# Attention and SwiGLU on one core: reordering the first batch's loads, preparations and products

## Chip, cores, metric

One core of a Trainium2 chip. The time is the device time of one execution in microseconds (us), median over executions. A profile's span is about 1.7 us shorter than the time of the same execution.

## The reference

Causal attention with a forget-like bias for 8 batches of 8 heads (576 positions, head size 64), then a SwiGLU block on the 4608 rows of 512 that result:

```python
scores = scale * np.matmul(q, k.transpose(0, 1, 3, 2))
cum = np.cumsum(np.maximum(s, 0.0), axis=-1)
bias = -(cum[:, :, :, None] - cum[:, :, None, :])
scores = np.where(causal, -1000000000.0, scores + np.minimum(bias, 0.0))
attn = softmax(scores)                      # exp of the maximum taken off, over the sum
x = np.matmul(attn, v) -> (4608, 512)
out = (silu(x @ w_gate) * (x @ w_val)) @ w_out      # 512 -> 1536 -> 512
```

## The kernel before

Heads come in 16 blocks of four ("block 2" is heads 8 to 11). A block is loaded as f32, cast to bf16, transposed by TensorE (blocks 0 to 4; later ones go through a DMA transpose) and copied from PSUM into `KQ`. A head then takes four score pieces (PE), exponentials (ACT), two causal selects (POOL), value products (PE), a division (DVE), and per pair of heads a transpose into `xt`. The heads of batch 0 run first, alone. From then on FFN tile `tt` and the heads of batch `tt+1` are interleaved step by step by `pump`. `SP` issues most loads, POOL the weight loads.

```python
def second_psum():                 # after the first batch: 2 wide + 4 single banks -> 8 single banks
    at_end = dict(released)
    first_psum.close()
    psb = ctx.enter_context(tc.tile_pool(name="psb", bufs=1, space=PSUM))
    ...

def side(h, step):                 # beside head 4*h+step
    bh = HB * h + step
    if bh == 8:  w_load("o", 0)
    if bh == 10: w_load("o", 1)
    if bh == H:                    # V of batch 1, f32 -> bf16, on POOL
        for c in range(5): cast_v(1, c, nc.gpsimd)
    ...
    if h + 2 < NHB and h + 2 >= NPE:
        if step == 1: cast_one(h + 2, "k", nc.gpsimd)
        if step == 2: cast_one(h + 2, "q", nc.gpsimd); scratch(h + 2)
        ...

def prep_one(hb, i):               # a quarter of a block: transposes, then two copies out of one bank
    g, nm = divmod(i, 2)
    nm = ("k", "q")[nm]
    pe_transpose(hb, nm, g)
    pe_out(hb, nm, g, 0, nc.vector)
    pe_out(hb, nm, g, 1, nc.scalar)

def first_batch():
    avq = {4: (0,), 5: (1, 2), 6: (3, 4), 7: (5, 6, 7)}
    wq = {0: ("g", 0), 1: ("v", 0), 3: ("g", 1), 5: ("v", 1)}
    for h in range(H):
        for ci in range(4): score_piece(h, ci)
        if h in wq: w_load(*wq[h])
        ...                        # block 1's transposes at h == 1, V 0's casts at h == 2 and 3
        for p in avq.get(h, ()):
            av_piece(p, range(NCH)); av_out(p)
            if p % 2 == 0 and p: x_pe(p // 2 - 1)
    ...
    load_v(1, range(5)); load_qk(3); load_qk(4)
    x_pe(H // 2 - 1)

hook = {                           # FFN tile 0, by step
    1: [lambda: cast_one(2, "k", nc.gpsimd), lambda: cast_one(2, "q", nc.vector)],
    2: [lambda: prep_one(2, 0)], ..., 5: [lambda: prep_one(2, 3)],
    8: [casts of block 3 on gpsimd], 21: [lambda: load_qk(5)],
}
n0 = 7 if tt == 0 else 0           # heads of batch 1 start after this step
```

The softmax here doesn't subtract the row's maximum and nothing guards it: scores larger than these inputs give would overflow.

## Time and profile before

| | us |
|---|---|
| median (3 runs, 407.97 to 409.79) | 408.16 |
| span of the profiled run | 406.5 |
| first score / first FFN matmul / last matmul's end | 11.93 / 34.40 / 402.78 |
| lost by TensorE: 34.40 to 46.5 / 46.5 to 65 / 65 to 75 / from 75 on | 4.2 / 4.15 / 0 / 4.45 |

"Lost" is the length of a stage less the time which its matmuls need at full clock, back to back; the prediction tells how the need was worked out. It counts half-clock time and small waits that "busy" hides. The lines themselves are in the prediction.

### The profile page before, as it was taken

Reading aid. Unit: us, or ns where it says so; the run is one execution under the profiler, and the core shown is the slowest. Engines: PE = TensorE matmul, PEld = TensorE weight load, DVE = VectorE, ACT = ScalarE, POOL = GpSimd, SP = SyncE. Lnnn points to the kernel's source line nnn. Section 1 sums busy time; section 2 is a strip of 40 time slices with the busy share of each in tenths; the row PEclk is TensorE's granted clock in tenths of the full one; section 3 lists DMA queues with packets and bytes.
Section 4 is the critical chain, followed back from the end, with each engine's and each line's share of the span. In section 5 each row is a group of like instructions: output and inputs, shape, how many; then the busy total and the mean of one; then the engine's idle time right before and its main releaser. Section 6 shows DMA issues by size and latency. Waiting matters only on the chain.

```text
span 406.5 us, 8052 instructions
## 1 busy us (share of the span) xinstructions
PE 384.8 (95%) x3100; PEld 213.0 (52%) x3100; DVE 249.1 (61%) x487; ACT 212.0 (52%) x407; POOL 125.0 (31%) x225
## 2 busy tenths in 40 slices
PE   2778799999999999999999999999999999999996
PEld 2664355655555555555555555555555554444442
DVE  7755658547863696368835784489447733852760
ACT  6742566855555655555545654655555542322321
POOL 6852444732442235222613162316211110000000
PEclk9988899999999999999999999999999999999999
DMA  7999899398635784579356944681510002002002
GB/s 242 188 250 212 267 192 269 133 272 190 178 93 194 174 206 118 173 194 211 102 157 192 247 72 127 214 167 51 120 57 0 2 27 78 0 16 89 2 1 103
DMA packets 85288, 56.71 MB, mean 140 GB/s; under 512 B 65489, under 2 KB 69553, under 8 KB 85249
## 3 DMA queue, kind: packets, MB, share of 16 engines
q1 hardware_dynamic: 81440, 51.44, 47.0%
q0 software_dynamic: 3808, 4.76, 6.9%
q8 instruction: 24, 0.39, 0.4%
q14 instruction: 16, 0.12, 0.1%
HBM read 37.90 MB, written 15.93 MB: 132 GB/s over the span
## 4 chain that ended last, share of the span: by engine, by line
PE 89%; DVE 4%; ACT 2%; DMA 2%; POOL 1%; issue 1%; ACTq 0%; SPq 0%
PE bank L546 23%; PE bank L518 22%; PE bank L533 22%; PE bank L347 9%; PE bank L385 7%; PE bank L420 3%; PE wide L347 1%; DMA kq<-HL 1%; PE one L385 1%; DMA s_sb<-in_s_dram 1%; ACT th L523 1%; POOL vt L171 1%; DVE pp L525 1%; DVE kq L301 1%; ACT pt L360 1%
## 5 line engine op out<-in xcount | busy, mean ns | idle before, releaser
L360 ACT ACTIVATE pt<-bank 128x512 bf16<-128x512 f32 x224 | 104.2, 505 | 42.4 <-PE bank L347 35.1
L525 DVE SCALAR_TENSOR_TENSOR pp<-th,bank 128x512 bf16<-128x512 bf16 x108 | 74.2, 687 | 65.2 <-ACT th L523 64.6
L518 PE MATMUL bank<-xt,wg 128*128 128x512 bf16 x432 | 112.1, 382 | 0.7 <-DVE xt L425 0.7
L533 PE MATMUL bank<-xt,wv 128*128 128x512 bf16 x432 | 112.5, 383 | 0.0
L523 ACT ACTIVATE th<-bank 128x512 bf16<-128x512 f32 x108 | 64.5, 597 | 81.6 <-PE bank L518 79.8
L546 PE MATMUL bank<-wo,ht 128*128 128x512 bf16 x432 | 105.7, 379 | 0.0
L363 POOL TENSOR_SCALAR_AFFINE_SELECT pt<-pt 128x512 bf16<-128x512 bf16 x64 | 40.8, 638 | 127.1 <-ACT pt L360 124.7
L538 DVE TENSOR_TENSOR ht<-pp,bank 128x512 bf16<-128x512 bf16 x108 | 73.8, 684 | 7.4
L347 PE MATMUL bank<-kq 128*128 128x128 bf16 (+4 forms) x504 | 66.7, 241 | 3.3 <-DVE kq L301 2.5
L347 PEld LDWEIGHTS <-kq 128*128 128x128 bf16 x576 | 46.1, 100 | 40.2 <-issue 4.2
L518 PEld LDWEIGHTS <-wg 128*128 128x128 bf16 x432 | 38.6, 98 | 36.9 <-issue 1.9
L533 PEld LDWEIGHTS <-wv 128*128 128x128 bf16 x432 | 38.9, 99 | 35.2 <-issue 1.7
L546 PEld LDWEIGHTS <-ht 128*128 128x128 bf16 x432 | 38.1, 98 | 34.9
L385 PEld LDWEIGHTS <-pt 128*128 128x128 bf16 x960 | 41.1, 98 | 19.0 <-issue 1.9
L385 PE MATMUL bank<-vt,pt 128*128 128x65 bf16 x840 | 44.0, 194 | 0.0
L554 ACT ACTIVATE ysb<-bank 128x512 f32<-128x512 f32 x36 | 21.5, 597 | 42.9 <-PE bank L546 41.4
L368 POOL TENSOR_SCALAR_AFFINE_SELECT pt<-pt 128x64 bf16<-128x64 bf16 x64 | 15.3, 239 | 63.4 <-ACT pt L360 60.7
L402 DVE TENSOR_TENSOR ot<-bank,rc 128x320 bf16<-128x320 f32 x56 | 27.5, 492 | 1.9
L424 DVE COPY xt<-bank 128x128 bf16<-128x128 bf16 (+6 forms) x28 | 9.0, 321 | 31.7 <-PE bank L420 31.0
L401 DVE RECIPROCAL rc<-bank 128x5 f32<-128x5 f32 x56 | 10.6, 190 | 25.2 <-PE bank L385 25.2
L171 POOL CAST vt<-rawv 128x512 bf16<-128x512 f32 (+1 forms) x40 | 25.8, 673 | 0.0
L230 POOL CAST ck<-rawk 128x1152 bf16<-128x1152 f32 x15 | 17.4, 1159 | 11.5 <-DMA rawk<-in_k_dram 11.5
(59 smaller groups left out, 191.6 us busy)
## 6 DMA issues: line engine op xcount, KB each, us to landing
out_dram<-ysb SPq DMA_DIRECT2D x36, 256.0 KB
rawk<-in_k_dram SPq DMA_DIRECT2D x15, 576.0 KB
rawq<-in_q_dram SPq DMA_DIRECT2D x15, 576.0 KB
rawv<-in_v_dram SPq DMA_DIRECT2D x32, 256.0 KB
ks<-ck SPq DMA_DIRECT2D x11, 288.0 KB
qs<-cq SPq DMA_DIRECT2D x11, 288.0 KB
wg<-in_moe_w_gate_dram POOLq DMA_DIRECT2D x2, 768.0 KB, 12.0
wv<-in_moe_w_val_dram POOLq DMA_DIRECT2D x2, 768.0 KB, 13.6
```

The source lines that it names most:

```text
L171: eng.tensor_copy(VT[b % 2][0:n, c, :, 0:D], loaded["v", b][0:n, c, :, :])
L347: nc.tensor.matmul(sc[:, o : o + w], T[:, 1, e * S + 128 * tj : e * S + 128 * (tj + 1)], T[:, 0, e * S + lo : e * S + hi], start=True, sto ...
L360: nc.scalar.activation(pt[:, c0 : c0 + W], sc[:, 0:W], AF.Exp, scale=0.125)
L363: nc.gpsimd.affine_select(pt[:, 1088:1600], pt[:, 1088:1600], pattern=[[0, 4], [1, 128]], compare_op=ALU.is_ge, fill=zreg, base=0, channel ...
L385: nc.tensor.matmul(av[:, bi * (D + 1) : (bi + 1) * (D + 1)], pt[:, c0 : c0 + 128], VT[b % 2][:, tj, h, :], start=(tj == 0), stop=(tj == bi),)
L402: nc.vector.tensor_mul(ot[:, :, e * D : (e + 1) * D], av3[:, :, 0:D], rc[:, :, None].to_broadcast([128, NCH, D]),)
L518: nc.tensor.matmul(pg, WG[j][:, c, f0 : f0 + 128], xt[:, c, :], start=(c == 0), stop=(c == 3),)
L523: nc.scalar.activation(th, pg, AF.Tanh, scale=0.5)
L525: nc.vector.scalar_tensor_tensor(pp, in0=th, scalar=1.0, in1=pg, op0=ALU.add, op1=ALU.mult)
L533: nc.tensor.matmul(pv, WV[j][:, c, f0 : f0 + 128], xt[:, c, :], start=(c == 0), stop=(c == 3),)
L538: nc.vector.tensor_mul(ht, pp, pv)
L546: nc.tensor.matmul(py, hts[ft][:, ts_ * 128 : (ts_ + 1) * 128], WO[ft // WKO][:, ft % WKO, :], start=(ft == 0), stop=(ft == NFT - 1),)
```

## The change

The intent is to bring the first batch's work into a better order, so that TensorE has no long wait ahead of its steady part: (1) weight loads later, behind V 0, in halves; (2) k and q of block 3 loaded ahead of V 1; (3) heads 0 to 5 score before the first value product, and in the next batch the value products follow the scores by up to three heads; (4) half of block 2 is prepared in the first batch; smaller: casts and memsets shared out otherwise, score rows of later blocks issued by POOL, stores one step later. Its core:

```diff
         def first_batch():
-            avq = {4: (0,), 5: (1, 2), 6: (3, 4), 7: (5, 6, 7)}
-            wq = {0: ("g", 0), 1: ("v", 0), 3: ("g", 1), 5: ("v", 1)}
+            avq = {5: (0,), 6: (1, 2), 7: (3,)}
+            wq = {
+                2: (("g", 0, 0), ("v", 0, 0)),
+                3: (("g", 0, 1), ("v", 0, 1)),
+                5: (("g", 1),),
+                6: (("v", 1),),
+            }
@@ (V 0's casts: c 0 to 2 on POOL at h == 3, c 3 and 4 on DVE at h == 1)
+                    load_qk(3)
+                if h == 6:
+                    cast_one(2, "k", nc.gpsimd)
+                if h == 7:
+                    aug(3, SP4)
+                    load_v(1, range(5))
+                    load_qk(4)
@@
+            cast_one(2, "q", nc.gpsimd)
+            w_load("o", 0)
+            w_load("o", 1)
+            x_pe(0)
+            for p in (4, 5, 6, 7):
+                av_piece(p, range(NCH))
+                av_out(p)
+                ...
+                if p >= 6:
+                    nm = ("k", "q")[p - 6]
+                    pe_transpose(2, nm, 0)
+                    for r in range(2):
+                        pe_out(2, nm, 0, r, nc.scalar)
+            x_pe(3)
@@
-            1: [lambda: cast_one(2, "k", nc.gpsimd), lambda: cast_one(2, "q", nc.vector)],
-            2: [lambda: prep_one(2, 0)],
-            3: [lambda: prep_one(2, 1)],
-            4: [lambda: prep_one(2, 2)],
-            5: [lambda: prep_one(2, 3)],
+            1: [lambda: prep_one(2, 2)],
+            2: [lambda: prep_one(2, 3)],
@@
-            n0 = 7 if tt == 0 else 0
+            n0 = 4 if tt == 0 else 0
@@ side()
-            if bh == 8:
-                w_load("o", 0)
-            if bh == 10:
-                w_load("o", 1)
-            if bh == H:
+            if bh == H + 2:
                 for c in range(5):
                     cast_v(1, c, nc.gpsimd)
@@ attn_items()
+        AV_AT = {H: (), H + 1: (), H + 2: (), H + 3: (H,), H + 4: (H + 1, H + 2), H + 5: (H + 3, H + 4)}
```

More of the change, by code (lines that the diff above doesn't have):

```diff
@@ L95 @@
     s_sb = const.tile([BH, S], FP32)
-    one_s = const.tile([BH, S], FP32)
+    one_s = const.tile([128, 1], FP32)
     c8 = const.tile([BH, S], FP32)
@@ L190, with init_vt @@
         nc.sync.dma_start(s_sb, s.rearrange("b h n -> (b h) n"))
+        def init_vt(i):
+            nc.gpsimd.memset(VT[i][:, :, :, D : D + 1], 1.0)
+            nc.gpsimd.memset(VT[i][64:128, 4, :, 0:D], 0.0)
         for r in range(NR):
@@ L196 @@
         nc.vector.memset(warm, 0.0)
+        nc.vector.memset(one_s, 1.0)
         nc.scalar.activation(warm, warm, AF.Exp)
-        nc.vector.memset(one_s, 1.0)
         nc.vector.memset(HL[:, 0:2, 0, :].bitcast(FP32), ONES2)
@@ L201, with pads @@
         make_identity(nc, ident)
+        def pads(i):
+            for r in range(2):
+                nc.gpsimd.memset(KQ[i][r][64 * r : 64 * r + 64, :, NR * S :], 0.0)
         for r in range(2):
-            nc.gpsimd.memset(aug_rows(0, r), 0.0)
+            nc.gpsimd.memset(aug_rows(0, r)[:, 1, :], 0.0)
             nc.scalar.mul(
-                KQ[1][r][64 * (1 - r) : 64 * (1 - r) + 64, 0, :],
-                one_s[:, 0:1].to_broadcast([64, NR * S + 64]), 0.0,
-            )
-        for r in range(2):
-            nc.gpsimd.memset(aug_rows(1, r)[:, 1, :], 0.0)
-            for i in range(2):
-                nc.gpsimd.memset(KQ[i][r][64 * r : 64 * r + 64, :, NR * S :], 0.0)
+                KQ[0][r][64 * (1 - r) : 64 * (1 - r) + 64, 0, :],
+                one_s[0:64, 0:1].to_broadcast([64, NR * S + 64]), 0.0,
+            )
+        pads(0)
+        init_vt(0)
+        init_vt(1)
+        nc.vector.memset(aug_rows(1, 0), 0.0)
+        nc.gpsimd.memset(aug_rows(1, 1), 0.0)
+        pads(1)
         nc.vector.tensor_scalar(s_sb, s_sb, 0.0, 8.0, ALU.max, ALU.mult)
-        nc.vector.tensor_tensor_scan(c8, one_s, s_sb, 0.0, ALU.mult, ALU.add)
+        nc.vector.tensor_tensor_scan(
+            c8, one_s[0:BH, 0:1].to_broadcast([BH, S]), s_sb, 0.0, ALU.mult, ALU.add
+        )
         nc.vector.tensor_copy(HL[:, 0, 1, :], c8)
@@ L219 @@
         SP4 = [nc.sync] * 4
+        GP4 = [nc.gpsimd] * 4
         cts = {}
@@ L304, in pe_out, with w_load @@
                 give(tp[1])
-        def w_load(kind, j):
+        def w_load(kind, j, h=None):
             dst = {"g": WG, "v": WV, "o": WO}[kind][j]
@@ L313, in w_load @@
                 w = moe_w_gate if kind == "g" else moe_w_val
-                src_ap = w[:, j * WCH : (j + 1) * WCH].rearrange("(c p) n -> p c n", p=128)
+                lo, hi = (0, WCH) if h is None else (h * WCH // 2, (h + 1) * WCH // 2)
+                src_ap = w[:, j * WCH + lo : j * WCH + hi].rearrange("(c p) n -> p c n", p=128)
+                dst = dst[:, :, lo:hi]
             nc.gpsimd.dma_start(dst, src_ap)
@@ L408, in av_out, with x_tiles @@
             pts.pop(bh)
+        def x_tiles(b, r):
+            for tt in ((0, 1) if b == 0 else (b + 1,)):
+                if r == 0:
+                    xts[tt] = xtp.tile([128, 4, TT], BF16, tag="xt", name="xt")
         def x_pe(pr):
@@ L412, in x_pe @@
             ot = ots.pop(pr)
-            for tt in ((0, 1) if b == 0 else (b + 1,)):
-                if r == 0:
-                    xts[tt] = xtp.tile([128, 4, TT], BF16, tag="xt", name="xt")
+            x_tiles(b, r)
             bs = take()
@@ L440, in side @@
                 if step == 0:
+                    transposes(h + 1)
+                    aug(h + 1, GP4)
+                if step == 2:
                     split(h + 1, "k", nc.vector)
-                    aug(h + 1, SP4)
-                if step == 1:
+                if step == 3:
                     split(h + 1, "q", nc.vector)
@@ L449, in side @@
                     cast_one(h + 2, "q", nc.gpsimd)
+                if step == 3:
                     scratch(h + 2)
-                if step == 3:
-                    transposes(h + 2)
             bn = h // 2 + 1
@@ L475, in prep_one @@
             pe_out(hb, nm, g, 1, nc.scalar)
-        PREP_AT = {(0, 3): 0, (1, 3): 1, (2, 1): 2, (2, 3): 3}
+        PREP_AT = {
+            2: {(1, 3): 0, (2, 1): 1, (2, 3): 2, (3, 1): 3},
+            3: {(0, 3): 0, (1, 3): 1, (2, 1): 2, (2, 3): 3},
+        }
+        AV_AT = {H: (), H + 1: (), H + 2: (), H + 3: (H,), H + 4: (H + 1, H + 2), H + 5: (H + 3, H + 4)}
+        X_AT = {H + 3: (), H + 5: (H + 1,), H + 6: (H + 3,), H + 7: (H + 5,)}
         def attn_items():
@@ L486, in attn_items @@
                     if step == 0 and 3 < h + 1 < NPE:
-                        aug(h + 1, SP4)
+                        aug(h + 1, GP4)
                     for ci in range(4):
@@ L492, in attn_items @@
                         yield kk + 0.1 + ci / 8
-                        if h + 1 < NPE and (step, ci) in PREP_AT:
-                            prep_one(h + 1, PREP_AT[step, ci])
+                        if (step, ci) in PREP_AT.get(h, ()):
+                            prep_one(h + 1, PREP_AT[h][step, ci])
                             yield kk + 0.1 + ci / 8
-                x = kk - 2
-                if x >= H and x % 2 == 1:
-                    x_pe(x // 2)
-                    yield kk + 0.5
-                p = kk - 1
-                if H <= p < BH:
-                    av_piece(p, (0, 1, 2))
-                    yield kk + 0.6
-                    av_piece(p, (3,))
-                    yield kk + 0.7
-                    av_piece(p, (4,))
-                    av_out(p)
-                    yield kk + 0.8
+                for x in X_AT.get(kk, (kk - 2,)):
+                    if x % 2 == 1 and H <= x < BH:
+                        x_pe(x // 2)
+                        yield kk + 0.5
+                for p in AV_AT.get(kk, (kk - 1,)):
+                    if H <= p < BH:
+                        av_piece(p, (0, 1, 2))
+                        yield kk + 0.6
+                        av_piece(p, (3,))
+                        yield kk + 0.7
+                        av_piece(p, (4,))
+                        av_out(p)
+                        yield kk + 0.8
+        stores = []
         def ffn_items(tt):
@@ L512, in ffn_items @@
             hts = []
+            for f in stores:
+                f()
+            stores.clear()
             for ft in range(NFT):
@@ L555, in ffn_items @@
                 give(ybs)
-                nc.sync.dma_start(
-                    out[tt * TT + ts_ * 128 : tt * TT + (ts_ + 1) * 128, :], ysb
-                )
+                for f in stores:
+                    f()
+                stores.clear()
+                stores.append(
+                    lambda a=tt * TT + ts_ * 128, y=ysb: nc.sync.dma_start(
+                        out[a : a + 128, :], y
+                    )
+                )
+                if tt == NTT - 1:
+                    stores.pop()()
                 yield 1
-        def init_vt(i):
-            nc.gpsimd.memset(VT[i][:, :, :, D : D + 1], 1.0)
-            nc.gpsimd.memset(VT[i][64:128, 4, :, 0:D], 0.0)
         cast_half(0, "k", 0, nc.scalar)
-        cast_half(0, "q", 0, nc.gpsimd)
+        cast_half(0, "q", 0, nc.scalar)
         aug(0, SP4)
@@ L569 @@
         load_qk(2)
-        aug(1, [nc.gpsimd] * 4)
         for nm in ("k", "q"):
@@ L576 @@
         pe_out(0, "q", 0, 0, nc.vector)
-        pe_out(0, "q", 1, 0, nc.scalar)
+        pe_out(0, "q", 1, 0, nc.vector)
         cast_half(0, "k", 1, nc.scalar)
-        cast_half(0, "q", 1, nc.vector)
+        cast_half(0, "q", 1, nc.gpsimd)
+        aug(1, GP4)
         for nm, eng in (("k", nc.scalar), ("q", nc.vector)):
@@ L583 @@
                 pe_out(0, nm, g, 1, eng)
-        cast_one(1, "k", nc.gpsimd)
+        cast_one(1, "k", nc.vector)
         cast_one(1, "q", nc.vector)
-        init_vt(0)
         def first_batch():
-            avq = {4: (0,), 5: (1, 2), 6: (3, 4), 7: (5, 6, 7)}
-            wq = {0: ("g", 0), 1: ("v", 0), 3: ("g", 1), 5: ("v", 1)}
+            avq = {5: (0,), 6: (1, 2), 7: (3,)}
[4 more added lines that the diff above has]
+                6: (("v", 1),),
+            }
             for h in range(H):
@@ L593, in first_batch @@
                     score_piece(h, ci)
-                if h in wq:
-                    w_load(*wq[h])
+                for w in wq.get(h, ()):
+                    w_load(*w)
                 if h == 1:
@@ L602, in first_batch @@
                             pe_out(1, nm, g, r, nc.vector)
-                if h == 2:
+                    for c in range(3, 5):
+                        cast_v(0, c, nc.vector)
+                if h == 3:
                     for c in range(3):
                         cast_v(0, c, nc.gpsimd)
-                if h == 3:
-                    for c in range(3, 5):
-                        cast_v(0, c, nc.gpsimd)
                     aug(2, SP4)
+                    load_qk(3)
[5 more added lines that the diff above has]
+                    load_qk(4)
                 for p in avq.get(h, ()):
@@ L612, in first_batch @@
                     av_out(p)
-                    if p % 2 == 0 and p:
-                        x_pe(p // 2 - 1)
-            init_vt(1)
-            aug(3, SP4)
-            load_v(1, range(5))
-            load_qk(3)
-            load_qk(4)
-            x_pe(H // 2 - 1)
+            cast_one(2, "q", nc.gpsimd)
[4 more added lines that the diff above has]
+                av_piece(p, range(NCH))
+                av_out(p)
+                if p == 5:
+                    x_pe(1)
+                if p == 6:
+                    x_pe(2)
+                if p >= 6:
+                    nm = ("k", "q")[p - 6]
+                    pe_transpose(2, nm, 0)
+                    for r in range(2):
+                        pe_out(2, nm, 0, r, nc.scalar)
+            x_pe(3)
         first_batch()
@@ L632, in pump @@
                     state["pos"] = 1e9
-        LAG = 1.65
+        LAGS = [0] + [1.65] * NTT
         hook = {
-            1: [lambda: cast_one(2, "k", nc.gpsimd), lambda: cast_one(2, "q", nc.vector)],
-            2: [lambda: prep_one(2, 0)],
-            3: [lambda: prep_one(2, 1)],
-            4: [lambda: prep_one(2, 2)],
-            5: [lambda: prep_one(2, 3)],
-            8: [lambda: cast_one(3, "k", nc.gpsimd), lambda: cast_one(3, "q", nc.gpsimd)],
+            1: [lambda: prep_one(2, 2)],
+            2: [lambda: prep_one(2, 3)],
+            7: [lambda: cast_one(3, "k", nc.gpsimd), lambda: cast_one(3, "q", nc.gpsimd)],
             21: [lambda: load_qk(5)],
@@ L644 @@
         for tt in range(NTT):
-            lo = H * (tt + 1) + (LAG if tt else 0)
-            hi = min(H * (tt + 2) + LAG, BH + 2)
+            lo = H * (tt + 1) + LAGS[tt]
+            hi = min(H * (tt + 2) + LAGS[tt + 1], BH + 2)
             span = 36
-            n0 = 7 if tt == 0 else 0
+            n0 = 4 if tt == 0 else 0
             n = 0
```

## The prediction

> **What bounds the kernel now.** I read the page's slices first, then busy time by stage, then what TensorE waited for, then the timelines of PE and POOL over the first 60 us. The slices say where to look:
>
> ```profile
> PE   2778799999999999999999999999999999999996
> POOL 6852444732442235222613162316211110000000
> PEclk9988899999999999999999999999999999999999
> DMA  7999899398635784579356944681510002002002
> ```
>
> A slice is about 10.2 us. PE is under 90% only in slices 1 to 5 and the last, and PEclk is low in 3 to 5. The stages, cut at the first score (11.93), the first FFN matmul (34.40) and the end of the long wait (46.51):
>
> ```profile
> core 0: us, PE busy (x) PEld busy (x) DVE busy (x) ACT busy (x) POOL busy (x), PEclk, DMA share, GB/s
> 11.93:34.40 22.47, 15.97 (x231) 12.66 (x232) 15.04 (x35) 12.52 (x16) 15.56 (x31) 0.92 1.15 230
> 34.40:46.51 12.11, 9.59 (x51) 4.39 (x51) 6.69 (x11) 4.03 (x7) 1.15 (x1) 0.87 1.04 266
> 46.51:65.00 18.49, 17.06 (x141) 9.88 (x142) 11.62 (x20) 12.94 (x26) 10.91 (x17) 0.91 1.00 191
> 75.00:402.80 327.80, 327.75 (x2543) 176.14 (x2541) 199.61 (x393) 166.56 (x334) 84.59 (x150) 1.00 0.45 120
> ```
>
> From 75 us on TensorE has no gap. Busy is not the same as full speed, so I took starts instead: in the steady part each kind of matmul starts a fixed time after the last one (512 columns 0.216 us, 128 columns 0.056, the 65-column value product 0.029). Multiplying these by the counts in each stage gives the time that the work needs at full speed. From 34.40 to the last matmul's end (402.78) are 368.4 us for 355.6 us of need: 12.8 us are lost, 4.5 of them spread over 75 to 403 (1.4%) and 8.3 between 34.40 and 65 (4.2 to 46.51, 4.1 after). Between 12 and 34.40 the need is 11.4 us out of 22.4. So what can be won is ahead of 65 us; afterwards TensorE's own work sets the end. The waits of PE from 34.3 to 75:
>
> ```profile
> PE bank L347 <- DVE kq L301: 2.5, 1, 2.5
> PE bank L518 <- DVE xt L425: 0.7, 1, 0.7
> PE bank L347 <- DVE pp L525: 0.6, 1, 0.6
> PE bank L272 <- DVE ot L402: 0.4, 1, 0.4
> PE bank L420 <- DVE ot L402: 0.3, 1, 0.3
> ```
>
> One wait, 2.5 us at head 8's first score, stands out: k and q of head block 2 are cast only after the first batch (at 32.6 on POOL and 37.6 on DVE), then go through four transposes and eight copies that alternate with the FFN's DVE work. The first batch itself is paced by a chain over POOL and PE:
>
> ```profile
> 20.84 0.76 POOL L315 DMA_DIRECT2D wg<-in_moe_w_gate_dram  x1
> 21.60 1.18 POOL L171 CAST vt<-rawv 128x512 bf16<-128x512 f32 x2
> ...
> 30.86 0.64 POOL L363 TENSOR_SCALAR_AFFINE_SELECT pt<-pt 128x512 bf16<-128x512 bf16 x1 [2.02 <-ACT pt L360]
> 31.44 0.24 POOL L368 TENSOR_SCALAR_AFFINE_SELECT pt<-pt 128x64 bf16<-128x64 bf16 x1
> ```
> ```profile
> 22.28 0.31 PE L385 MATMUL one<-vt,pt 128*128 128x65 bf16 x5 [1.77 <-POOL vt L171]
> 22.83 0.19 PE L385 MATMUL one<-vt,pt 128*128 128x65 bf16 x1 [0.24 <-POOL vt L171]
> ...
> 34.40 1.86 PE L518 MATMUL bank<-xt,wg 128*128 128x512 bf16 x4 [0.70 <-DVE xt L425]
> 36.06 1.74 PE L533 MATMUL bank<-xt,wv 128*128 128x512 bf16 x4
> ...
> 37.92 1.03 PE L518 MATMUL bank<-xt,wg 128*128 128x512 bf16 x4
> ```
>
> The V casts stand behind a weight issue on POOL; the value product of head 0 waits for them and, in PE's order, holds the scores of head 5 back; so ACT idles 2.0, 1.85 and 1.3 us before the last three pairs of exponentials (PE's turn alternates with value products), and the last causal select ends at 31.7. From there to the FFN's first matmul are 2.7 us (value product, DVE, transpose, DVE). That first pair of matmul groups then takes 1.66 us each from start to start, against 0.86 later.
>
> [...] three spans of 3.41 us at half clock, from 23.9, 34.1 and 47.7, each after a stretch in which PE worked about half the time or less. At full demand such a window costs up to 1.7 us. [...] DMA share is 1.15 in the first batch, and the third issue of V 1 takes 4.3 us on SP while the weights are moving.
>
> **The change, part by part.** (a) Start: POOL's cast of q goes to ACT, one cast of k to DVE, memsets are shared out. The first score waits for the chain s load, five DVE operations to 8.16, 3.6 us of DMA, so it stays at 11.9; 0 us.
>
> (b) First batch. Order on PE: heads 0 to 5 score before the first value product. ACT, at 1.64 us a head from 13.0, can run to head 5's end at about 23. POOL then becomes the pace, because it now issues six weight DMAs, not four (halves cost an issue each, 0.78), and casts k of block 2 (1.15) before head 7's select. I add its list: three selects to 18.4; two issues to 20.0; select of head 3 to 20.85; two issues to 22.4; three V casts (0.58 each) to 24.2; selects 4 and 5 to 25.9; issue 26.6, select 6 27.5, issue 28.2, cast k 29.4, select 7 30.2. Head 6's scores stand behind value product 0, thus behind 24.2; its exponentials run 25.1 to 26.7 and head 7's to about 28.8, so POOL, not ACT, ends last. With the same 2.7 us tail the FFN starts at 33.0, **1.4 us earlier**. The weights' first halves, issued at 18.4 and 19.2, need 0.4 MB each at the 115 to 200 GB/s seen: before 28, not in the way.
>
> (c) Block 2: half of its transposes (10 x 0.056 = 0.56 us of need) moves into the batch's idle PE time: **0.6 us**. Its casts are done before the FFN, the other half is at the FFN's first two steps, and head 8 scores after the fifth step, about 5 us in. DVE and ACT copies (0.7 each, one after the other here) with tanh and products between them end at about +4.6 us. The 2.5 us wait goes, and with it the half-clock window that followed at 47.7 (1.7): **4.2 us**.
>
> (d) Value products of heads 8 to 12 come three heads later, so PE no longer meets `ot` and the select closely: the waits of 0.4 and 0.3 go, some of the 0.6 may. Against that, scores take banks sooner: I reckon that the third gate product waits some 0.7 us for a bank held until DVE's product. In the gate and value part of this tile I add DVE 12 x 1.37 + 6 x 0.77 + 5 x 0.7 + 1.2 = 25.7 us beside about 28.5 of PE, so about a microsecond more of small waits is likely. Net **0.5 us**.
>
> (e) FFN's opening at half clock costs 1.5 us now. PE is denser in front of it in the new order, but still waits for the last select; even odds: **0.75 us**.
>
> (f) Later: score rows issued from POOL, stores one step later, transposes given one step more. No PE wait there now, so 0.
>
> Sum: 1.4 + 0.6 + 4.2 + 0.5 + 0.75 = 7.45, with 0.3 for the rest of the 8.3: 7.75. 408.16 - 7.75 = 400.4 us, 1.9% less.
>
> **Rivals.** *A new wait in front of the FFN.* POOL gets 14.5 us of work between 13 and 30.2 and hardly idles; if an issue or cast runs longer, FFN starts as late as before and the gain is only (c) to (e), some 402 to 403. For it: POOL's order; against: the durations are steady in the trace.
>
> *V 1 or a weight arrives late.* wo is now issued at 32, not at 49 and 58, behind wg 1 and wv 1, and takes engines from V 1, which crept while weights moved (issued 30.7, last piece at 43). I put V 1 at about 48 and its use, value product of head 8, at about 53; k and q 4 follow at some 50. If V 1 takes until 55, PE stops 2 to 3 us: 403 to 405. wv 1 is due at 47 and should land by 44.
>
> *Full gain.* Clock stays full at the FFN's opening and no bank wait appears: 397 to 398.
>
> *Steady state.* If POOL's extra issues or the later splits open gaps after 75 us, the gain is eaten; DVE has 61% and POOL 26% load there, so I give it little.
>
> **Range and chances.** 400.4, with 397.0 for the full gain and 404.0 for a late transfer. The 2% line is at 400.0, just beside the middle: faster 0.45, same 0.53, slower 0.02.
>
> **What would show it right or wrong.** In the new profile: first score still at 11.9 (a); POOL without idle from 18.4 to 30 and FFN's first matmul near 33.0 (b); PE's wait for DVE `kq` gone and half-clock windows down from three to one or two (c, e); no wait on `rawv`, `wv` or `rawk` that reaches PE in 35 to 65 us; from 70 us the same 1.4% loss. A first FFN matmul after 34, a PE wait over 1 us between 35 and 65, or a gap after 75 would make it wrong on the slow side; an FFN start before 32 on the fast side.

## The result

405.15 us median (4 runs, 405.01 to 405.92) against 408.28 us for the kernel before on the same chip. The ratio is 0.992, interval 0.9892 to 0.9947: about 3 us less, where 7.75 were predicted, and outside the range. (Ratios here and below are the mean time of one kernel's runs over that of the other's of the same rounds, so not quite the ratio of the medians.)

The page's slices of the changed kernel:

```profile
PE   3777989999999999999999999999999999999996
PEclk9999999999999999999999999999999999999999
```

PEclk has no dip any more, where it had 8s in slices 3 to 5. That is the profiled execution, with a granted clock of 0.999; the other three have 0.995, which is worth about one half-clock window of 3.4 us more (0.4% of 403 us lost), and where that one fell isn't recorded. PE's 8 in slice 6 (about 50 to 60 us) is a hollow in the FFN, behind the first batch. The stages from this kernel's own first FFN matmul on; columns are those of the stages in the prediction (length, busy time and count for PE, weight loads, DVE, ACT and POOL, then clock, DMA share, GB/s):

```profile
34.95:46.50 11.55, 11.14 (x75) 6.08 (x75) 7.21 (x12) 7.59 (x15) 3.71 (x6) 1.00 1.18 200
46.50:65.00 18.50, 16.33 (x141) 9.14 (x139) 12.15 (x23) 12.31 (x25) 10.45 (x19) 1.00 1.13 229
65.00:75.00 10.00, 9.54 (x110) 6.12 (x108) 7.31 (x18) 6.93 (x14) 3.81 (x7) 1.00 0.72 252
```

| | before | after | predicted change | measured change |
|---|---|---|---|---|
| first FFN matmul | 34.40 | 34.95 | -1.4 | +0.55 |
| need of PE from there on | 355.6 | 355.0 | -0.6 | -0.6 |
| lost from there to 46.5 | 4.2 | 0.6 | | -3.6 |
| lost, 46.5 to 65 | 4.15 | 3.75 | | -0.4 |
| lost, 65 to 75 | 0.0 | 0.9 | | +0.9 |
| lost from 75 on | 4.45 | 4.45 | 0 | 0.0 |
| loss after the FFN's start in all | 12.8 | 9.7 | -5.75 | -3.1 |
| end of the last matmul | 402.8 | 399.7 | -7.75 | -3.1 |

So the wait before head 8 and the half-clock windows went as intended, but the FFN started later instead of earlier, and between 46.5 and 75 the loss is larger than it was. What PE waited for from 34.9 to 75 us, from the view of waits:

```profile
PE bank L545 <- ACT kq L313: 1.4, 1, 1.4
...
PE bank L560 <- DVE pp L552: 0.7, 1, 0.7
...
PE bank L401 <- ACT pt L376: 0.4, 1, 0.4
```

The first line is new. It is best seen in the timelines around the FFN's start. ACT copies the first half of block 2 out of PSUM, four copies of 0.75 us:

```profile
31.88 3.02 ACT L313 COPY kq<-one 64x640 bf16<-64x640 bf16 x4 [2.70 <-DVE ot L418]
```

DVE finishes `xt`, the FFN's input, at 34.15:

```profile
33.74 0.41 DVE L444 COPY xt<-one 128x512 bf16<-128x512 bf16 x1
```

and PE starts the FFN not then but 0.05 us after ACT's last copy (34.90):

```profile
34.95 1.02 PE L545 MATMUL bank<-xt,wg 128*128 128x512 bf16 x4 [1.35 <-ACT kq L313]
```

That matmul does not read what ACT copies. It is the first to write into the second PSUM pool, which opens when everything that used the first pool is done, and the trace has ACT's semaphore among those that it waits for (in e2 below, without the change of pool, it has not).

The second piece, the hollow at 50 to 55 us, is a chain over three engines. DVE, ACT and PE, each from its timeline:

```profile
50.58 0.81 DVE L315 COPY kq<-bank 64x640 bf16<-64x640 bf16 x1
53.44 0.69 DVE L552 SCALAR_TENSOR_TENSOR pp<-th,bank 128x512 bf16<-128x512 bf16 x1 [2.04 <-ACT th L550]
```

```profile
51.43 0.75 ACT L313 COPY kq<-bank 64x640 bf16<-64x640 bf16 x1 [1.78 <-DVE kq L315]
52.20 0.71 ACT L376 ACTIVATE pt<-bank 128x512 bf16<-128x512 f32 x2
52.80 0.60 ACT L550 ACTIVATE th<-bank 128x512 bf16<-128x512 f32 x1
```

```profile
54.17 1.02 PE L560 MATMUL bank<-xt,wv 128*128 128x512 bf16 x4 [0.72 <-DVE pp L552]
```

One bank of block 3's transposes is emptied by DVE (to 51.39) and only then by ACT; the program makes ACT's copy wait for DVE's. ACT stands at that copy for 1.78 us; its exponentials and the tanh start only after it (52.20 and 52.80), so DVE gets its next product 2.04 us late, and PE waits 0.72 for the bank.

The third: V 1, predicted to land at about 48. Of its five casts in POOL's timeline the third waits 4.35 us for the load, and the last ends at 57.4:

```profile
54.84 0.62 POOL L171 CAST vt<-rawv 128x512 bf16<-128x512 f32 x1 [4.35 <-DMA rawv<-in_v_dram]
...
56.79 0.61 POOL L171 CAST vt<-rawv 64x512 bf16<-64x512 f32 x1 [0.22 <-DMA rawv<-in_v_dram]
```

### The profile page after: what moved, and what is told of

Read it like the earlier page. It is cut to its first block, busy times and chain, and to the rows that moved or that the text cites.

```text
span 403.4 us, 8053 instructions
## 1 busy us (share of the span) xinstructions
PE 383.0 (95%) x3100; PEld 212.8 (53%) x3100; DVE 244.4 (61%) x488; ACT 213.6 (53%) x409; POOL 154.4 (38%) x272
## 4 chain that ended last, share of the span: by engine, by line
PE 83%; DMA 7%; SPq 5%; POOL 2%; DVE 1%; ACT 1%; issue 0%; POOLq 0%; ACTq 0%
PE bank L573 22%; PE bank L545 21%; PE bank L560 21%; PE bank L363 8%; PE bank L401 6%; SPq L164 5%; DMA rawv<-in_v_dram 3%; PE bank L439 2%; DMA rawk<-in_k_dram 2%; PE wide L363 1%; DMA kq<-HL 1%; POOL vt L171 1%; DMA s_sb<-in_s_dram 1%; ACT pt L376 1%; PE one L286 0%; PE one L401 0%
## 5 line engine op out<-in xcount | busy, mean ns | idle before, releaser
L545 PE MATMUL bank<-xt,wg 128*128 128x512 bf16 x432 | 111.0, 379 | 1.8 <-ACT kq L313 1.4
L560 PE MATMUL bank<-xt,wv 128*128 128x512 bf16 x432 | 110.9, 379 | 0.7 <-DVE pp L552 0.7
L565 DVE TENSOR_TENSOR ht<-pp,bank 128x512 bf16<-128x512 bf16 x108 | 73.8, 683 | 6.5 <-PE bank L545 0.5
L545 PEld LDWEIGHTS <-wg 128*128 128x128 bf16 x432 | 38.5, 98 | 37.7 <-issue 1.9
L401 PEld LDWEIGHTS <-pt 128*128 128x128 bf16 x960 | 40.2, 97 | 20.8 <-issue 2.4
L581 ACT ACTIVATE ysb<-bank 128x512 f32<-128x512 f32 x36 | 21.5, 597 | 44.4 <-PE bank L573 43.1
L185 POOL DMA_DIRECT2D kq<-HL x52 | 30.6, 589 | 1.1
L384 POOL TENSOR_SCALAR_AFFINE_SELECT pt<-pt 128x64 bf16<-128x64 bf16 x64 | 18.1, 282 | 32.9 <-ACT pt L376 32.3
L443 DVE COPY xt<-bank 128x128 bf16<-128x128 bf16 (+6 forms) x28 | 8.9, 319 | 32.2 <-PE bank L439 27.3
L171 POOL CAST vt<-rawv 128x512 bf16<-128x512 f32 (+1 forms) x38 | 24.8, 678 | 5.1 <-DMA rawv<-in_v_dram 5.1
```

What stands on the lines that cost most here:

```text
L171: eng.tensor_copy(VT[b % 2][0:n, c, :, 0:D], loaded["v", b][0:n, c, :, :])
L185: engs[hh].dma_start(KQ[hb % 2][r][r0 : r0 + 4, :, e * S : (e + 1) * S], HL[bh : bh + 1, :, :, :],)
L401: nc.tensor.matmul(av[:, bi * (D + 1) : (bi + 1) * (D + 1)], pt[:, c0 : c0 + 128], VT[b % 2][:, tj, h, :], start=(tj == 0), stop=(tj == bi),)
L545: nc.tensor.matmul(pg, WG[j][:, c, f0 : f0 + 128], xt[:, c, :], start=(c == 0), stop=(c == 3),)
L560: nc.tensor.matmul(pv, WV[j][:, c, f0 : f0 + 128], xt[:, c, :], start=(c == 0), stop=(c == 3),)
L565: nc.vector.tensor_mul(ht, pp, pv)
```

## The experiments

Times are medians; "loss" is as defined above. Line numbers shift by a few lines from kernel to kernel. Unless said otherwise an edit is made to the changed kernel. A profile shows one execution, and not always a typical one: those of e1 and e6 were the fastest of their kernels (407.13 and 403.59 us), those of e4 and e14 lay 1.8 and 1.5 us above the median (406.60 and 405.70), so their last column and their waits needn't hold for the median.

| run | median us | ratio to before | FFN's first matmul minus first score | loss 46.5-65 / 65-75 |
|---|---|---|---|---|
| before | 408.16 | 1 | 22.5 | 4.15 / 0 |
| changed | 405.15 | 0.992 | 23.6 | 3.75 / 0.9 |
| e1_wo_late | 409.29 | 1.0016 | 23.0 | 3.8 / 4.6 |
| e2_one_pool | 403.89 | 0.9887 | 21.9 | 5.7 / 0.3 |
| e3_both | 409.01 | 1.0012 | 22.6 | 3.9 / 4.6 |
| e4_cast_first | 404.77 | 0.9907 | 21.7 | 7.8 / 0.2 |
| e5_wo_mid | 405.29 | 0.993 | 21.7 | 3.9 / 2.1 |
| e6_one_engine | 404.46 | 0.9912 | 23.4 | 3.0 / 1.2 |
| e7_block2_back | 407.80 | 0.9984 | 22.4 | 3.9 / 0.8 |
| e8_three | 405.97 | 0.9934 | 21.7 | 1.0 / 7.5 |
| e9_no_wo1 (wrong result) | 399.78 | 0.9779 | 23.4 | 0.6 / 0.3 |
| e10_whole_weights | 404.86 | 0.9911 | 22.4 | 3.75 / 0.3 |
| e11_wo_at_10 | 406.82 | 0.9949 | 22.6 | 0.9 / 5.7 |
| e12_xt_on_act | 406.86 | 0.995 | 21.5 | 0.8 / 6.3 |
| e13_k5_late | 399.59 | 0.9772 | 21.75 | 0.8 / 0.3 |
| e14_k5_alone | 404.22 | 0.9891 | 21.8 | 7.2 / 0.3 |

Intervals are about plus or minus 0.002 to 0.0035. The fourth column is from one profile each and is to be read with care: the batch's code is the same in the changed kernel, e1 and e14, and it took 23.6, 23.0 and 21.8 us. In the changed kernel PE was at half clock until 16.9 us, in e1 until 14.3, in e14 to 10.3.

### e1_wo_late: is it V 1?

```diff
-            w_load("o", 0)          # end of first_batch
-            w_load("o", 1)
+            if bh == H + 3:         # side()
+                w_load("o", 0)
+            if bh == H + 4:
+                w_load("o", 1)
```

> The changed kernel with the two wo loads moved from the end of the first batch to heads 11 and 12, after V 1's casts. Theory A (V 1 starves behind the weights, and its late cast stalls PE): the last V 1 cast ends at 45 to 49 us instead of 57.4, the loss of TensorE between 46.5 and 65 us falls from 3.75 to about 2, and the time from 405.15 to about 403.4. Rival (that loss is banks, DVE and ACT, whatever V 1 does): V 1 comes early, the loss stays at 3.5 or more, and the time stays within 0.5 us of the changed kernel.

V 1 came early (last cast ended 50.5), and yet the loss between 46.5 and 65 stayed at 3.8: theory A fell. But the time rose by 4 us, which neither side had expected: I had put the loads too late. PE's timeline shows both, the same 0.72 us wait as above and then the first of two waits for wo (4.0 us together):

```profile
52.49 1.02 PE L564 MATMUL bank<-xt,wv 128*128 128x512 bf16 x4 [0.72 <-DVE pp L556]
...
69.03 1.04 PE L577 MATMUL bank<-wo,ht 128*128 128x512 bf16 x4 [1.41 <-DMA wo<-in_moe_w_out_dram]
```

### e2_one_pool: is it the PSUM pool?

```diff
+        pss = ctx.enter_context(tc.tile_pool(name="pss", bufs=1, space=PSUM))
         psa = first_psum.enter_context(tc.tile_pool(name="psa", bufs=1, space=PSUM))
@@
-            bank["s", i] = psa.tile([128, 512], FP32, name=f"one{i}")
+            bank["s", i] = pss.tile([128, 512], FP32, name=f"one{i}")
@@ second_psum(): only the two wide tiles' pool is closed and reopened
+                    psb.tile([128, 512], FP32, name=f"bank{i}") if i < 4 else old["s", i - 4]
```

> The changed kernel with the four single PSUM banks kept over both phases, so that the first FFN matmul no longer waits for the whole first PSUM pool, thus for ACT's copies of block 2. Theory P (that pool change holds the FFN back): the first FFN matmul starts at 34.2 us or a little before instead of 34.95, and the time falls by 0.7 to 1.0 us to about 404.3. Rival (ACT's copies have to be done anyway before the tanh of step 1 and before head 8, so the wait only moves): the matmul starts earlier, other waits grow by as much, time within 0.3 us of the changed kernel.

403.89 us, 1.26 less than the changed kernel's median (ratio 0.9887 against 0.992): theory P holds, a little above its size. The first FFN matmul no longer waits for ACT, whose last copy of block 2 ends at 34.09 here:

```profile
32.68 1.06 PE L549 MATMUL bank<-xt,wg 128*128 128x512 bf16 x4
```

It even starts 0.6 us before the last `xt` copy ends (33.30); in the trace only the fourth matmul of the group waits for DVE.

### e3_both

Both edits together.

> Both edits (wo late and one PSUM pool). If A and P both hold and do not overlap, their gains add: about 402.6 us. If V 1's lateness or the pool wait only hides another limit (DVE and ACT in the first tile), less than the sum: 403.5 or more.

409.01 us, for the same late wo; it tells nothing about the sum.

### e4_cast_first: do V 0's casts pace the batch?

On the one-pool kernel; POOL's V 0 casts move ahead of the second pair of weight issues at head 3.

> The one-pool kernel with POOL's three casts of V 0 ahead of the second pair of weight issues. Theory (POOL's whole list up to head 7's select, and DVE's tail behind it, sets the FFN's start, not the moment of value product 0): value product 0 ends 1.5 us sooner (about 23.8), but the last select still ends at 30.6 and the FFN starts within 0.4 us of the one-pool kernel; same time within 0.4. Rival (the V casts are what paces the batch): FFN starts 1 to 1.5 us sooner than in the one-pool kernel, and the time falls by as much.

The batch took 21.7 us against 21.9, as the theory had it. But the two profiles have unlike clocks (half clock until 17.9 us here; until 12.3 and from 22.5 to 25.9 in e2), and value product 0 ended 13.1 us after the first score against 12.9, not 1.5 sooner, so what was to be tested didn't come about, and V 0's casts as the pace are not ruled out. The time is 0.9 us worse, where 0.4 at most was expected. In the profiled execution PE waited 2.2 us for V 1 and two half-clock windows (55.5 to 62.3) followed; that execution is the slowest of the seven, so this is not shown to be what the median lost.

### e5_wo_mid

One pool, and wo at heads 9 and 11.

> One PUSM pool, and the two wo loads at heads 9 and 11 (about 42 and 54 us): after V 1 has the engines to itself, but in time for the output products at 69 us. In the one-pool kernel value product 0 of batch 1 waited 1.1 us for late V 1 casts and a half-clock window (1.7 us at most) followed. If that is V 1's doing: no wait on the vt casts after 50 us, no wait on wo, and about 401.5 to 402.5 us against 403.89. If the stall around 52 to 58 us comes from DVE and ACT alone, as the first wo experiment suggests: within 0.5 us of 403.9.

405.29 us, which neither side had expected: V 1's wait went, the 0.72 and its neighbours stayed (loss 3.9), and a new wait of 1.8 us on a causal select appeared at 74 us. On POOL that select stood behind the cast of block 5's k, which had waited 7.6 us for its load (to 71.5); I saw what this meant only at e12.

### e6_one_engine: the copies out of one bank

```diff
-            pe_out(hb, nm, g, 0, nc.vector)
-            pe_out(hb, nm, g, 1, nc.scalar)
+            eng = nc.vector if nm == "k" else nc.scalar
+            pe_out(hb, nm, g, 0, eng)
+            pe_out(hb, nm, g, 1, eng)
```

> The changed kernel with each PSUM bank of transposed k or q emptied by one engine (k by DVE, q by ACT) instead of its two halves by DVE and then ACT. Theory D (ACT's copy waits in its queue behind DVE's of the same bank, and the tanh and exponentials behind it; that is most of the 3.75 us lost from 46.5 to 65): ACT's waits on DVE kq (10.1 us from 35 to 75) go to under 1, the loss falls to 2 to 2.7, time 403.6 to 404.2. Rival (ACT's sum of work is what limits there): the same loss, time within 0.4 of 405.15.

404.46 us (ratio 0.9912). ACT's waits on DVE's copies, 10.1 us in the changed kernel, are gone from its list. The loss from 46.5 to 65 is 3.0, but 2.3 of it is now a wait for V 1's casts, that the old stall had hidden:

```profile
PE bank L401 <- POOL vt L171: 2.3, 2, 1.9
```

The mechanism of theory D is shown. Its gain in time is not: 0.7 us by the medians, 0.3 by the ratios, executions from 403.59 to 405.81 beside 405.01 to 405.92.

### e7_block2_back: what block 2's early preparation is worth

The casts, transposes and copies of block 2 are put back into the FFN's steps 1 to 5, and the heads start at step 7.

> The changed kernel with the preparation of head block 2 put back as before (casts and all transposes in the FFN's steps 1 to 5, heads from step 7). My account gives it the whole gain after the FFN's start: the wait of 2 to 3 us before head 8's score comes back, with it the half-clock window, loss from the FFN's start to 65 us up from 4.3 to about 8; but the FFN starts 0.8 us sooner, since ACT's copies no longer stand before it. Sum: 407.5 to 409. Rival (what helped is the score-ahead order or the weights): 404.5 to 406.

407.80 us, as my account says. PE's wait before head 8 is back:

```profile
45.56 0.83 PE L363 MATMUL bank<-kq 128*128 128x128 bf16 x8 [1.28 <-DVE kq L315]
```

But it is half as long as in the kernel before. The larger part of the 4.0 us lost up to 46.5 lies in two half-clock windows at the FFN's opening (32.3 to 39.1), in front of that wait; none follows it here. The start is earlier after the first score (22.4), as ACT's copies no longer stand before it. This part of the change is worth 2.65 of its 3.1 us; that the half clock at the opening comes with it, and not by where the 3.4 us windows fell in that execution, is not shown by one profile (the four executions lie within 1 us).

### e8_three

One pool, wo at heads 9 and 11, one engine per bank.

> One pool, wo at heads 9 and 11, and one engine per bank together. If each removes its own wait: 400.5 to 401.5 us, less than 400 only if no half-clock window falls after 30 us. If they hide one another: 402 or more.

405.97 us, on the side of "they hide one another", and the most telling miss: from the FFN's start to 65 us only 0.95 us are lost (4.3 in the changed kernel), and then all of it is given back in one wait (PE's waits from 33 to 80):

```profile
PE bank L582 <- DMA wo<-in_moe_w_out_dram: 5.3, 1, 5.3
```

with two half-clock windows behind it. The second half of wo had been issued behind V 1 and a cast, at 56 us, and moved together with V 2 and blocks 5 and 6 (DMA share 1.17 from 50 to 60 us, 1.08 from 60 to 70).

Four profiles together tell what the 3.75 us between 46.5 and 65 are. With V 1 late the loss is 3.75 in the changed kernel, with two engines per bank, and 3.0 with one (e6); with V 1 early it is 3.9 with two (e5; 3.8 in e1) and 1.0 with one (e8). Either edit alone meets the other limit; both together take 2.75 us away.

### e9_no_wo1: less to transfer

On e8; the second half of wo is not loaded and the first is used twice, a wrong result.

> Wrong result on purpose: the kernel with three edits (one pool, wo in the middle, one engine per bank) without the load of wo's second half; the first half is read in its place, same matmuls. Theory T (the sum of the transfers up to about 72 us is what the later edits ran into; the DMA share is over 1 in every kernel from 20 to 70 us): taking 0.79 MB, thus about 4 us of engine time, away removes the 5.3 us wait on wo and lets block 5's k land about 4 us sooner (cast at 65 to 67 instead of 69.3), loss from 65 to 75 us falls from 7.5 to under 1.5, time about 399 to 400.5. Rival (only that one late issue was badly placed, POOL's selects or banks then take over): the wo wait goes but others of 2 us or more stand in 60 to 80, time 402 or more.

399.78 us: theory T's number. From the FFN's start to 75 us 0.9 us are lost. What one load of 0.79 MB costs there is 6 us, more than its 4 us of transfer (an estimate, at the 200 GB/s or so that the traces show). One thing in the expectation was wrong: the DMA share isn't over 1 in every kernel from 20 to 70 us, the kernel before has 0.85 from 40 to 50.

### e10_whole_weights: the weight loads put back

```diff
-            wq = {2: (("g", 0, 0), ("v", 0, 0)), 3: (("g", 0, 1), ("v", 0, 1)), 5: (("g", 1),), 6: (("v", 1),)}
+            wq = {0: (("g", 0),), 1: (("v", 0),), 3: (("g", 1),), 5: (("v", 1),)}
```

> The changed kernel with the weight loads of the first batch back as before: whole, at heads 0, 1, 3 and 5. POOL issues two fewer, so V's casts come about 0.8 us sooner and head 7's select about 1.5; but ACT's copies of block 2 (they need POOL's cast of q) and the pool change still hold the FFN's first matmul: my account gives a start 0.3 to 1 us sooner after the first score, V 1 earlier because the weights finish earlier, and about 404.2 to 405.2. Rival (the load order of the change is what gains: V 0 and block 2 land later beside the weights, and stall): V 0's casts wait on DMA, FFN starts 1 us or more later, 406 or more.

404.86 us, the same as the changed kernel within the spread: issuing the weights behind V 0 and in halves, the change's first item, neither gains nor costs (one of its six executions took 408.18). V 1's last cast still ended at 56.3. In the profile the first batch itself is shorter, under a like clock (half clock until 17.2 us, 16.9 in the changed kernel): from the first score to the last select 17.3 us instead of 19.3, to `xt` 21.6 instead of 22.8. So the later loads, with POOL's two issues more, did hold the batch up; a half-clock window behind it (34.3 to 37.7) took most of that back. The first FFN matmul waits for ACT's copies here too (1.35 us).

### e11_wo_at_10 and e12_xt_on_act

Both have one pool and one engine per bank, and issue wo right behind V 1's casts. e12 also takes the `xt` copies of the first two pairs from DVE to ACT.

> One pool, one engine per bank, and both wo loads right behind V 1's casts (about 48 us). If placing is all: no wait on wo (lands by 62), V 1's casts done by 50.5, loss from the FFN's start to 75 us about 2.5, time 401 to 402. If the transfers' sum is the floor: block 5's k is cast at 70 or later, a select behind it holds PE for 1 to 4 us between 66 and 76, time 402.5 to 404.5.

> The same with the copies into xt of the first two head pairs on ACT (idle there from 29 to 31.5) instead of DVE, which works without a gap from 28.4 to 32. If DVE's queue sets the batch's end: last value product 0.5 to 1 us sooner, the FFN starts 0.5 to 1 us sooner after the first score. Time: as much less if nothing later binds; the same as the run before it if the transfers do.

406.82 and 406.86 us, worse than the floor theory's own number. The e12 batch is the shortest of all (21.5 us), but time does not show it, and the copies on ACT can't be credited with it: the batch of e11 (22.6) had a half-clock span from 23.4 to 26.8 that e12's had not. wo no longer stalls anything; instead POOL does, in e12 at the cast of block 5's k, which lands at 71 us:

```profile
58.77 0.64 POOL L383 TENSOR_SCALAR_AFFINE_SELECT pt<-pt 128x512 bf16<-128x512 bf16 x1 [1.68 <-ACT pt L380]
71.04 1.14 POOL L248 CAST ck<-rawk 128x1152 bf16<-128x1152 f32 x1 [11.63 <-DMA rawk<-in_k_dram]
...
73.25 0.24 POOL L388 TENSOR_SCALAR_AFFINE_SELECT pt<-pt 128x64 bf16<-128x64 bf16 x1
```

The L388 select in the last line belongs to head 13, beside which the cast was put; ACT had ended that head's exponentials by 62 us. It stands behind the cast, and PE stands behind it:

```profile
PE one L405 <- POOL pt L388: 5.4, 1, 5.4
```

### e13_k5_late and e14_k5_alone: only POOL's order

```diff
-                if step == 1:
+                if step == (3 if h == 3 else 1):
                     cast_one(h + 2, "k", nc.gpsimd)
-                if step == 2:
+                if step == (3 if h == 3 else 2):
                     cast_one(h + 2, "q", nc.gpsimd)
```

e13 is e12 with this, e14 the changed kernel with this alone.

> The run with one pool, one engine per bank, wo behind V 1 and xt on ACT, and the casts of block 5 moved from heads 13 and 14 to head 15. In the run without this, POOL stood 11.6 us at the cast for block 5's k, which lands at 71, and a causal select of an earlier head behind it held TensorE for 5.4 us. If that queue order is what turns the transfers' sum into a stall: the wait of 5.4 us and the two half-clock windows go, loss from 65 to 75 us under 1.5, first 75 us as good as in the run without wo's second half, time 398 to 400. If the late transfers themselves bind (V 2, block 5 needed soon): a new PE wait of 2 us or more between 60 and 95 us, time 402 or more.

> The changed kernel with that one edit alone. There POOL stood 6.2 us at block 5's k, but PE waited only 0.5 us on the select behind it, since it was late itself. Expected: the loss of 0.9 us between 65 and 75 falls to 0.3 or less, time 404.3 to 405.0. If the edit is worth its 5 us by itself: 401 or less.

e13: 399.59 us, ratio 0.9772 (0.9742 to 0.9801), correct; it beats both kernels, the changed one by 1.4% of the medians; whether it is 2% below the kernel before is unclear, as the interval takes in 0.98. Against e12 it is 7.3 us for one edit, the 5.4 us wait and the two half-clock windows (71.0 to 77.8) that came with it. Nothing is left out of its transfers; block 5's k was cast at 73.4. PE's waits from 34 to 80 are two, a 0.2 and

```profile
PE one L405 <- POOL pt L388: 0.3, 1, 0.3
```

and the two stages that lost most, 46.5 to 65 and 65 to 75, read

```profile
46.50:65.00 18.50, 18.16 (x191) 11.18 (x190) 15.54 (x31) 14.41 (x28) 11.16 (x19) 1.00 1.04 200
65.00:75.00 10.00, 10.00 (x99) 6.01 (x98) 4.02 (x11) 6.88 (x13) 4.74 (x9) 1.00 0.76 256
```

PE is full but for 0.34 us, at full clock. So the transfers themselves did not bind: what turned them into a stall was one cast, waiting for a late load, in front of selects in POOL's queue. Theory T, which e9 had seemed to confirm, falls in its plain form. In e8 two things came late almost together, wo's second half (landed 70.4) and the select behind block 5's k (cast at 69.3, select's end 71.7); leaving a load out took the first away and brought the second forward (k cast at 66.4).

e14: the loss from 65 to 75 fell to 0.3 as expected, and the time to 404.22, just under the range given. In the profiled execution (405.70) the batch was short (no half clock after 10.3 us), so that PE came earlier to the value product of head 8, and V 1 was not ready:

```profile
53.86 0.47 PE L401 MATMUL bank<-vt,pt 128*128 128x65 bf16 x9 [0.44 <-ACT pt L376]
56.29 0.21 PE L401 MATMUL bank<-vt,pt 128*128 128x65 bf16 x1 [1.96 <-POOL vt L171]
```

Two half-clock windows (54.7 to 61.5) followed, and 7.2 us were lost. In this kernel, by these two profiles, an FFN that starts earlier waits longer for V 1 (start 34.95, no wait; start 32.65, 2.0 us).

## Why the prediction was wrong, by its own steps

**(a) Start.** Put at 0; the first score came at 11.38 instead of 11.93. Over all profiles it varied from 10.3 to 11.9, so this is no gain that can be claimed.

**(b) "With the same 2.7 us tail the FFN starts at 33.0, 1.4 us earlier".** This step failed: 34.95, and counted from the first score 23.6 us instead of 21.1. The 2.5 us are three terms:

- *The pool, 0.65 us.* One part was left out: the first FFN matmul waits for the whole first PSUM pool, and the change had put four ACT copies at the end of that pool. I did see those copies and had them done by 33.8, but did not ask what their end releases. In every profile that has both, the FFN starts 0.05 us after the last of them, 0.8 after `xt` (e1, e6, e10, e14 as well); in the kernel before it was 0.15 after `xt`. e2 measured the cost in time, 1.26 us.
- *The rest of the tail, 1.0 us.* Value product 7 started 1.0 us after the last select's end, not 0.03 as before: on PE it stood behind a transpose that had waited for DVE's division and behind block 2's transposes, and DVE worked through five heads' divisions without a gap from 28.4. So the tail was 4.3 us, not 2.7.
- *POOL's list, 1.0 us.* The last select's end, 30.6, looks close to the predicted 30.2, but this is the luck of the earlier first score: from there it is 19.25 us, not 18.3. The profiled run was at half clock until 16.9 us, which may be the reason; but e10, at half clock until 17.2, had the select at 17.3 with two issues fewer.

Nor does POOL's list alone set the end. In e7 and e8 the last select ended 17.7 and 17.5 us after the first score, and `xt` was ready only 22.3 us after it, as in the kernel before (22.3; 22.8 in the changed kernel). The 1.4 us don't show under a like clock: e3, with half clock to 14.0 and from 24.2 to 27.7 (before: to 13.6 and from 23.9 to 27.3), took 23.3 to `xt`. The shortest were 21.0 in e14, with no half clock after 10.3, and 21.6 in e10. How much of the batch's length is clock and how much is order stays open.

**(c) "4.2 us".** Right. The wait of 2.5 us went, and so did the window behind it. e7 brought back a wait of 1.3 us, with half-clock windows in front of it and not behind, and cost 2.65 us with an earlier FFN start set against it.

**(d) "Net 0.5 us".** The step that failed by most: I had "about a microsecond more of small waits", and with the windows gone 3.75 + 0.9 us are lost from 46.5 to 75. Before, about 1.6 of the 4.15 us lost there were the window at 47.7 (3.4 us long, with matmuls worth 1.8), so small waits rose from about 2.6 to 4.65 us, by 2.1 instead of falling by 0.5. The term was mis-sized because I added DVE's work and PE's work, and saw room, but not that the two copies out of one bank follow each other on two engines, with ACT's tanh behind the second. e6 took the order away, and e8, where V 1 was early too, lost 1.0 us in that stage. The wait for a bank forecast at the third gate product, some 0.7 us, came at the fourth with 0.4 us (`bank L545 <- DVE ht L565` in the view of waits); the 0.72 us at the eighth value product was not seen coming.

**(e) Clock.** Better than the even odds: no half-clock window at the FFN's opening in the changed kernel, 1.5 us. e10, with the same batch but for the loads, had one, so this is luck as far as is known.

**(f) Later stages.** Right: 4.44 against 4.45 us lost after 75.

**The rivals.** "A new wait in front of the FFN" was named, with the wrong engine (POOL's list; it was ACT and the pool). "V 1 or a weight arrives late" came near in time (403 to 405) and had the right event: V 1's last cast ended at 57.4, where I had put its landing at about 48. But e1 shows that it was not what cost the 3.75 us in this run: with V 1 early, the same loss stood there, so that its time came near is luck. V 1 is a second limit right behind the first, and it binds as soon as the first is gone (e2, e4, e6, e14).

Why V 1 was so late: counting the trace's DMA packets in 2 us slices from 34 to 52, the two queues moved the same number (235 and 234 from 36 to 38), but weights at 173 GB/s and V 1 at 30, since V comes in 256-byte pieces and the weights in 1536-byte ones. In the kernel before, once the weights were through, the same pieces moved at 199 to 211 GB/s (38 to 42). What makes the counts equal isn't shown by the trace. I had taken V 1's pace from the kernel before, where the weights ended at 39, and not asked what two more weight loads in front of their end do to small packets. e1, without them, had V 1's last cast done at 50.5; e10, with the other weights early again, at 56.3.

**What stays open.** e13 is five edits away from the changed kernel and was run as a whole; how its 5.6 us divide among pool, copies, wo's place, `xt` and block 5 is not known beyond the single runs, which do not add up. By their medians, one pool gives about 1.3, one engine per bank 0.7 (within the spread), block 5 alone 0.9, with overlap through V 1; on top of the other four, block 5's casts were worth 7.3 (e12 to e13).

## What to carry to other kernels

When one wait in such a chain of engines is removed, list what each engine reaches next and when its input lands, for the next two or three waits and not for the first alone: here five limits stood close behind one another (pool change, copies on two engines, V 1, wo, block 5's cast), and single edits measured 0 to 1.3 us, or a loss, where all together gave 5.6. In e12 POOL stood 11.6 us at a cast that waited for its load, and a select whose input was ready stood behind it, so a cast for later goes behind the selects needed now. And when a buffer pool is closed, ask who still reads from it: the first matmul into the new PSUM pool started 0.05 us after ACT's last copy out of the old one and 0.8 us after its own input, and keeping four banks open took 1.26 us off the median (e2).

## What the traces show of clock and queues

- In the kernel before the clock fell to half, for 3.41 us each, from 23.9, 34.1 and 47.7. In the 3.4 us before these PE was busy for 1.4, 1.8 and 1.2 us. The busy share alone doesn't tell, as the changed kernel kept full clock through 16.9 to 20.3 and 20.3 to 23.7 and after them, with 1.8 us busy in each. And in e14 and e4 the clock stayed at half for two windows (6.8 us) after waits of 2.0 and 2.2 us.
- How much a comparison can suffer: the first full-clock moment came at 10.3 us in e14, at 16.9 in the changed kernel and at 17.9 in e4, and the same code for the first batch (changed kernel, e1, e14) took 21.8 to 23.6 us (that the clock made this difference is argued, not tested).
- In the changed kernel V 1's 256-byte packets, beside weight packets of 1536 and later 1024 bytes, got 28 to 39 of about 200 GB/s, packet for packet, from 34 to 52 us.
- POOL stood 11.6 us at one cast (e12), with a select behind it whose input ACT had ended by 62 us, 9 us before the cast began.
